# A memory-recurrent transformer block: a planner that counts TensorE's instructions, and the first 16 recurrent steps cut into parts

## The chip, the core and the metric

The kernel runs on one core of a Trainium2 chip. The core has TensorE (matmuls, PE in the profile; its weight loads are PEld), VectorE (DVE), ScalarE (ACT), GpSimd (POOL) and SyncE (SP, which here issues nearly all DMAs). Each engine runs its own instructions in order and waits on semaphores for the others. TensorE can be cut into tiles (two of 64 rows, four of 32 columns, eight of 64 x 32), which work beside each other. Results go to PSUM, eight banks of 128 x 512 float32, and are copied from there to SBUF by ScalarE or VectorE. The metric is the device time of one execution in microseconds (us), as a median of runs.

## What is computed

Two layers, each an attention with a recurrent memory (A) followed by a gated MLP (B), with the same weights in both layers:

```python
for s in range(n_seg):                                  # 64 segments of 32 rows
    h = jnp.concatenate([mem, xs], axis=1)              # 8 memory rows + 32 rows of x
    q, k, v = (jnp.einsum('btd,dhe->bhte', h, W) for W in (Wq, Wk, Wv))   # 16 heads of 256, D = 448
    scores = jnp.where(mask, jnp.einsum('bhqe,bhke->bhqk', q, k) * scale, -1e9)
    o = jnp.einsum('bhte,hed->btd', jnp.einsum('bhqk,bhke->bhqe', softmax(scores), v), Wo)
    mem = o[:, :M, :]                                   # the next segment's memory
    outs.append(o[:, M:, :])
...
x = x + A(layernorm(x)); x = x + B(layernorm(x))        # B: (relu(x Wg) * (x Wu)) Wd, 1792 wide
x = x + A(layernorm(x)); x = x + B(layernorm(x))
```

The memory rows make the segments of a layer a chain: segment s + 1 cannot start its memory part before segment s has put out its eight memory rows.

## The kernel before

*Weights folded.* At the start the kernel multiplies Wq with Wk to `A` and Wv with Wo to `Bsb` for each head (`weights`, `values`, lines 828 and 842), so that a step needs the scores h A h' and the output P h B alone. The first two steps (`step < RAW`) use Wv and Wo one after the other (`unfused`), since `Bsb` isn't ready. The MLP's weights are loaded into the space that the staging of these weights leaves free (`glu_weights`: 18 loads, each of which waits for the one before it).

*The chain.* `chain(step)` is one step of the recurrence, for both layers at once: the second layer runs LAG = 7 segments behind the first, so that there are 70 steps. Step by step: the u pass (line 1021: two halves of 56 matmuls, 7 blocks x 4 column tiles x 2 row tiles, of `mT`, the transposed memory, with `A`); the copy of its four PSUM parts to `Usb`; `turn_u`, which transposes them on VectorE into `uT` (the last 32 columns by way of `tl`); `middle`: scores (line 1228), softmax, its transpose to `PTm` (507, 513), the y product (1286, 1289) and its copy to `YTm`; the output pass (line 1063: 56 matmuls of 448 columns in four column tiles, into one bank `bo`); its copy as a high and a low bfloat16 part, `Ohi` on ScalarE and `Olo` on VectorE, with a small copy of each; the column sums with `Sel` (line 493, 8 matmuls into the bank `br`), which give the transposed memory; and its copies to `mT` (one on VectorE, two across the halves of the partitions) and to `mC`, whose transpose `Rsb` goes to the memory rows of later segments by copies and DMAs. Other segments' rows ride along in the columns that the memory leaves free (`ride`, `single`, `third`; tiles `Tr`, `Pr`, `Tsb`).

*The rest of the work.* All other rows of the segments (`att_half`, `att_group`), the MLP (`glu_units`, `glu_down`) and the norms depend on the chain by the memory rows only. This work fills TensorE while a step's copies and softmax run.

*Who sets the order.* Every operation is recorded with what it reads and writes, a cost per engine and a priority (`_Sched.add`). TensorE's order is written out: `LINE` says, one sign per matmul group, which of the groups left comes next. The orders of the other engines, and which engine takes a copy that several may take (`EV`: ScalarE or VectorE), follow in `schedule()` from the planned times and priorities; `ORDER` shifts the priorities of parts. Where the plan sees a long hole on TensorE, it puts in dummy matmuls (`filler`, line 1646). A change of the tile shape costs `TURN` in the plan. `emit` writes out each engine's instructions with the waits.

Of the kernel before, what the change touches and what calls it, by code (L numbers as in the profile page):

```python
# [7 lines left out]
ACT = mybir.ActivationFunctionType  # L8
# [4 lines left out]
D = 448  # L13
# [3 lines left out]
M = 8  # L17
# [15 lines left out]
ORDER = ("rtaaaaRrjSAaQuLYRAnSb0LNYORXJTwUURBAoZFYxGIsOlyBLeuISxkqYlTuxwENNFHCQAvHZCKfIDDPxGVOqz0UgvrawGAaGoiaLCUaExvfad"  # L33
         "apaqZXakeoayYiaOYeYk0uvaahTxSJfZrbspHeSjbFsgCWHFsi00NtwfOraapajVAgpBxWpieejwMdTNGrdneahPhAIzaaraqrHfIpFMQpkxhC"
         "CcZZkDSqlpyOjQzgeHnQUhcuSapdaFmhKRdiOYlpiweLwTmPA0smp0JM0yggNJbZbTKZbfDNlluCEsJoSYVLqXjxxtjWPavwaZkADUurYfyFcq"
         "fkO0aVDSSVDLhdmLTjENTFZUoRixmDKTKaCaalbXJUbaNAosqbfRysAGdJDHgjAXgUSiugIKbjRFcMfkV0oxwbAjuwihxEaHjLXxAe0kIvNKaU"
         "datURQkpwEDKLvfzvSc0YIogTIaApWBDxUZJeNgmOJtkAXhjaZoaRCADL0LnFXXoujjvuSklKPoKBWwaXSOGFsQdAyPwKbhlUjkVqZRftprce0"
         "sSZoMXrRLmVXlac0aLSlIVcyMitQzKXyHLgcVPWyXgdgoKwHNodXtuYRLkSbrYuaAEabcvgehdwCVIHfiRrbgDCLkuYzcGZAgSTAAJmcynUVhk"
         "HVyeIEYlmbAgeixIMWfqccp0UvwwaLDaURdrT0sKsBd0OXyIoaUvOLUVtEuDaTKlwhOs0IDxsOKOSDaBOaeTWgzTRMfEwZlnGJZxPTLRgnPAcz"
         "pPBQyVXZgVLCFGybysTTGTh0mCnasZeIVJLcWhMbZfRaPDaNK0QMEBqrAXpkhODS0SZRhmQoKZJAGnpKlAZfVagMNVdHcaqsaMZiuKdQvwgmVj"  # L40
         "GFHUajftyotDaeMNKnYfbsoNMGdKptSpckDOFvzlRcjHjMhZJknKkfgUrdanHaZpYHaaXSzQuocWelk0EthLJTCBIlvuZygRbQqPoCYXjKaEda"
         "oNQIcpihSMTRhRAAsqTNXbjwwRSbmlJeFEyMrmhNtZtsmcNunW0Emio0hEayjLtmvrtYBkgaRXXabaxxY0IUKljBSaaaaaaQkHsKaXaaaaaaaa"
         "aaaaaaaaaaadII0lNPSanJakbnc")

SIGNS = "ABCDEFGHIJKLMNOPQRSTUVWXYZabcdefghijklmnopqrstuvwxyz0123456789+-*/=<>()[]{}.,:;!"
LINE = ("AAEACAABAHHFDDDBAAAAIHEDECBAABAJHHCEBDAAAIAIHDBBCAAAAHIHGCCAABAAHIHGDECCBAKAIHAEBCBAAIAPHoJHAABDCCAAAeAdABALCA"
        "XRAEUAKSA~bAQAPAnOAcMALAAJABHAGAgTBADXACABAAAGWAFSCEVQGAFUODGMACGJPGOOGCHFCFAHDMBECDBABAGAAABTAACCPASWBHJAXKAA"
        "IOAAAHOFAFAQPAABBLCQSAAIIACGGGHGH=SR6GXQYFPFCNAAAANJJJLKKJAIIAACFLAEADAAFGAAAAECAANBBLOYAAQAAHJRMAAAEEAODFAUUE"
        "=.aASFBBBOCAMAAAJJJ5JJKKAsJPAIHHAGGGAFBGGEADDAABGBAAAABCAAAAKYQAVdAIaJAHEPAAAGDDDAAMBBbaEBADCAUaAACRAQCBARNNNA"
        "ALAML43LRArJJBIBHHHAGAIHeAGAACDCCGAAAAADBAATMAAWWedKVAaJJfAvAtKcLKAAAElJVADDA44FF1CCz5GABBDAcsbrjChoooGAAlXADD"  # L50
        "jjAABgelLBVbb(b7AaaabKCZBXAXWGAATAYAAQEAOhOOOEDAOMFKAWLKFhEYHHAALFMRFWMLFFFiAQKFEAssHRHQDAmOIAAiGGgAjfffAAdAfe"
        "AEAZAZfAAXBA2UUAAARRRtRAzTSDBDDBAALAAAGHMAFFfFFFAHADAAPBCCBZYBoKPVL0KZBwMBWMLBBBFKFBEMBhDA=/FuEAB<8BEBB4ACk1bB"
        "ayyyAZfAuAAvuQ~BrirAwgPEnBmlACjjjkLANgGggfAAdjAAAaBRAXyGWWWCYCUCTUUTldCSAAZACUObDNCAAvDJJJEDWKVLKHAzyAFEANtAGA"
        "qvBpQFEmmmBBkkFAjjJFggAAGdC[c(cccdFAAZADCYYAAAVTAAYSRlRkAQQQRDQCCCBAAJAVbAAAfSdTjSbVFAQAEDQzZDAAKKBTBxILBBBFFB"
        "EAA=/DlCc9FiC*KCAB2WA0iAAxxxAAwvAvvukQbAqwhPPAAAkBoCimBhhhAgAgfQWDAbIgAAuY1YzYYYACXWAWqAVVU1DCAYREAADNrNTRCMMM"
        "LAMEJAm22EUUHDxA2AXuEAOEq~FDpppApCEmCDDlkAAAhDAAedBcAADZZZaAAXABAWWAAARSwoSRAVrQBCDDCBAJJJKAAAGAAARXAACbBiZBBL"
        "dLLBTZ5BMvB1MBBBILnMLBUqEAA**CJCC<8cABBA3k2kEDzzzAzAxAxxfAAuRArhqhpQsAnnnPCAlkElkBApiNYfBeAdAAAAZZZAAaYXAAWWDf"
        "DAASEAAPUOOUCCMMMAOAKDAH98CPOG4A9MAE0RzZ2yyyADOwvAvuUCCrAwKQEAEl;l:DkkkAFAihAihE4DeAdMAADAYDCWAAAAARRRSAgFDACA"
        "AAJAXAAAFAYofFRcRGFPEAQAATBYOKBVLBrNBBBLuVFBEAA<=fFC-CcA=B7BD5AlC2223kC10AAyyAAfvR0AVs,s.RvAqqqGqSoOBBDAjjAAhA"
        "AAejIAcHSHZZZAbAIWAjXXBBBA-TRYAAQAOOFRAMMMEASKR77DAHOA2BBaEZxADvPuuuvAAsAttAAJQpnAAAlAFji,AAgggD(EDAdFbAADDZZX"  # L60
        "AAAVAAAYSRmRkAQQQBACCNAALAJAVAaAAnnSedSSAETYQS0SzEEOAvDQVMALAvB2B0LKBBBFFIBrIH65EBZACCCFxCCA0u~LAtVQQqqq~CAqpP"
        "RooFCtmDCjaiCYgBAeeeKEAbbAbbFRCYeCCAVATTtCBRRRERmEEANAaFNNMcAAIAIOHDaGZGfCLFFFIIAQEADHsrDRGGAmABqkGLiAhhhFQAfA"
        "dDcdcAAAZDAAWbAAU0ATTTUAARASRxoAXQPrGCCMCLBBAIIIEEAFFACYRAAcBaiBNAeNMBAKZSKAK1A0KApIAAAIkIApDA--FICC7CA-a4AD2l"
        "1112kDzA0zAFATA1uAAsQqqiQooopAPPlmAAAllDhCAAgmAdmAdAbGaAKYYYZQYXAYnYYAAUAMTZSC+BQADO{DRNNNDNxMMAWVLAAAYRAYBAOF"
        "AMELLLMAEKJAIKJEAAGFAEADXDDDEAABLAOAHSGaAFBOAHTHHDJPDAAAFCEECGCABAHCCAAAAABCAFAGEEEADAAB")


class _Op:
    __slots__ = ("idx", "engs", "cost", "fn", "deps", "prio", "dma", "eng", "ndep", "users", "ready",
                 "start", "end", "need_inc", "val", "clock", "slot", "seq", "alloc", "mode",  # L70
                 "touch", "busy", "cross", "at", "also", "land", "side", "group")
# [1730 lines left out]
```

## Time and profile before

| | |
|---|---|
| median of 3 runs | 1491.38 us (1491.05 to 1492.07) |
| the profiled execution | 1486.13 us, of which the span from the first to the last instruction 1484.3 us |
| granted TensorE clock | 1.000 over the whole span |
| instructions | 79353 |
| VectorE, ScalarE, GpSimd busy | 78%, 62%, 12% of the span |
| matmuls | 35104, and as many weight loads |

A matmul is put down with the time from its start until its result is in PSUM, so that several overlap, and a busy TensorE need not be at its full rate. Idle time of an engine stands in square brackets with what ended it; "issue" is idle time in which the engine waited for nothing that the profile shows. Times in a timeline, and in the chain of waits, count from the start of the span.

### The profile page before, as it was taken

To read this page: it belongs to the slowest core of one execution; us is meant where nothing else is said; L and a number is where in the kernel's file an instruction comes from. 1 tells how busy PE (TensorE), PEld (TensorE's weight loads), DVE (VectorE), ACT (ScalarE), POOL (GpSimd) and SP (SyncE) were. 2 spreads that over 40 slices of the span, in tenths; PEclk is the share of its full clock that TensorE was granted. 3 is DMA by queue.
4 is the path that set the end of the run, shared out by engine and by line. 5 is a ranking of instruction groups with operands and counts; after the bars stand their busy time and mean duration, and the time that the engine had idled before them with its cause. 6 is when DMAs were issued, how large, how long until landed. Compare 5 with 4: busy or idle time off the path is not lost.

```text
span 1484.3 us, 79353 instructions
## 1 busy us (share of the span) xinstructions
PE 1459.1 (98%) x35104; PEld 1031.4 (69%) x35104; DVE 1151.0 (78%) x3862; ACT 915.4 (62%) x2635; POOL 179.6 (12%) x701
## 2 busy tenths in 40 slices
PE   9998999999999999999999999999999999999999
PEld 6555666677767776777768767677668676776676
DVE  6677777788877878687877878697887878778865
ACT  7766666676656667566656656575665657556553
POOL 3011111111111111011110111011110111011000
PEclk9999999999999999999999999999999999999999
DMA  9502200000000000000000000000000000000000
GB/s 275 152 26 65 59 8 9 9 9 8 9 4 14 9 8 15 4 17 5 18 4 14 8 11 11 4 18 5 17 5 8 14 11 12 4 11 5 11 9 12
DMA packets 64552, 34.00 MB, mean 23 GB/s; under 512 B 34112, under 2 KB 64080, under 8 KB 64208
## 3 DMA queue, kind: packets, MB, share of 16 engines
q1 hardware_dynamic: 63888, 28.65, 7.7%
q8 instruction: 276, 4.52, 1.3%
q14 instruction: 68, 0.56, 0.1%
q10 hardware_dynamic: 320, 0.26, 0.1%
HBM read 21.36 MB, written 1.84 MB: 16 GB/s over the span
## 4 chain that ended last, share of the span: by engine, by line
PE 92%; DVE 4%; ACT 1%; DMA 1%; issue 1%; SPq 1%; POOL 0%
PE psG L493 22%; PE psG L1374 15%; PE psC L1063 10%; PE psG L1581 9%; PE psC L1021 8%; PE psG L1021 5%; PE psG L1286 3%; PE psG L1063 2%; PE psG L1400 2%; PE psG L1610 2%; PE psG L842 2%; PE psC L1228 1%; PE psC L1286 1%; PE psC L493 1%; PE psG L828 1%; PE psC L1374 1%
## 5 line engine op out<-in xcount | busy, mean ns | idle before, releaser
L493 PE MATMUL psG<-Bsb,P 128*128 128x448 bf16 x1232 | 262.2, 353 | 0.0
L1374 PE MATMUL psG<-HT,A 64*128 64x128 bf16 x4388 | 254.9, 216 | 0.3 <-issue 0.3
L1374 PE MATMUL psG<-HX,A 64*128 64x128 bf16 x3291 | 238.6, 216 | 0.0
L1374 PEld LDWEIGHTS psG<-HT,A 64*128 64x128 bf16 x4388 | 210.5, 94 | 7.8 <-issue 2.3
L483 ACT ACTIVATE Ug<-psG 64x128 bf16<-64x128 f32 (+4 forms) x405 | 142.6, 369 | 61.1 <-PE psG L1374 35.8
L1374 PEld LDWEIGHTS psG<-HX,A 64*128 64x128 bf16 x3291 | 173.8, 94 | 0.0
L493 PEld LDWEIGHTS psG<-Bsb,P 128*128 128x128 bf16 x1232 | 107.2, 97 | 92.6 <-issue 9.3
L1063 PE MATMUL psC<-Bsb,YTm 128*32 128x448 bf16 x3080 | 156.0, 353 | 0.7 <-ACT YTm L483 0.4
L1212 DVE STREAM_TRANSPOSE uT<-Usb 128x384 bf16<-128x384 bf16 x280 | 144.3, 536 | 0.3 <-PE psC L1228 0.3
L1021 PE MATMUL psG<-A,mT 64*32 64x448 bf16 x4032 | 141.8, 350 | 1.4 <-ACT mT L483 0.5
L1021 PE MATMUL psC<-A,mT 64*32 64x448 bf16 x3808 | 136.6, 350 | 1.1 <-issue 0.9
L1581 PE MATMUL psG<-GG,glu 64*128 64x256 bf16 x2310 | 133.6, 269 | 0.0
L486 DVE CAST Ug<-psG 64x128 bf16<-64x128 f32 (+4 forms) x284 | 112.6, 407 | 19.8 <-PE psG L1374 8.5
L1581 PEld LDWEIGHTS psG<-GG,glu 64*128 64x128 bf16 x2310 | 111.6, 94 | 16.3 <-issue 1.5
L1063 PEld LDWEIGHTS psC<-Bsb,YTm 128*32 128x32 bf16 x3080 | 77.7, 97 | 61.5 <-issue 3.0
L483 ACT ACTIVATE P<-psG 128x448 bf16<-128x448 f32 x219 | 111.5, 543 | 7.5 <-PE psG L1289 2.6
L1021 PEld LDWEIGHTS psC<-A,mT 64*32 64x32 bf16 x3808 | 70.4, 92 | 51.5 <-ACT mT L483 5.6
L493 PE MATMUL psG<-glu,P 128*128 128x448 bf16 x434 | 94.2, 352 | 0.3 <-DMA glu<-in_B_W_down_dram 0.3
L1021 PEld LDWEIGHTS psG<-A,mT 64*32 64x32 bf16 x4032 | 74.1, 92 | 25.2 <-ACT mT L483 2.9
L1592 DVE TENSOR_TENSOR P<-P,psG 128x512 bf16<-128x512 bf16 x82 | 56.3, 686 | 41.6 <-ACT P L1591 41.2
L1591 ACT ACTIVATE P<-psG 128x512 bf16<-128x512 f32 x83 | 49.5, 596 | 62.6 <-PE psG L1581 56.0
L486 DVE CAST P<-psG 128x448 bf16<-128x448 f32 x130 | 78.8, 616 | 10.3 <-PE psG L1289 8.8
(282 smaller groups left out, 3160.9 us busy)
## 6 DMA issues: line engine op xcount, KB each, us to landing
Tsb<-Rsb SPq DMA_DIRECT2D x288, 1.5 KB
Tsb<-Rsb SPq DMA_DIRECT2D x288, 2.0 KB
HR<-xn SPq DMA_DIRECT2D x128, 32.0 KB, 1.9
Bsb<-in_A_Wq_dram SPq DMA_DIRECT2D x6, 384.0 KB, 6.8
Bsb<-in_A_Wk_dram SPq DMA_DIRECT2D x6, 384.0 KB, 6.3
HR<-Rsb SPq DMA_DIRECT2D x126, 1.5 KB
HR<-Rsb SPq DMA_DIRECT2D x126, 2.0 KB
X<-in_A_x_dram SPq DMA_DIRECT2D x16, 112.0 KB, 3.2
```

The source lines that it names most:

```text
L483: return E.activation(out, i, ACT.Copy, scale=1.0 if scale is None else scale)
L486: return E.tensor_copy(out, i)
L493: return E.matmul(out, lhsT=lhsT, rhs=rhs, **k)
L842: i = E.matmul(bk.ap()[row0:row0 + mn, to:to + of.stop - of.start], lhsT=lhs[:, et, m0:m0 + mn], rhs=rhs[:, et, of], start=(et == 0), stop ...
L1021: i = E.matmul(ub[v].ap()[32 * j:32 * j + 32, 0:D], lhsT=self.mT[rw, WHERE[b], first:first + 32], rhs=cols, start=(b == 0), stop=(b == 6), ...
L1063: x = E.matmul(bo.ap()[32 * j:32 * j + 32, 0:D], lhsT=self.YTm[:, q, :], rhs=self.Bsb[:, chunks[q], :], start=(i == 0), stop=(i == 13), ti ...
L1212: self.s.add("dve", 560, busy=486.0, fn=lambda E, e, v=v, of=of: E.transpose(outs[:, 2 * v:2 * v + 2], of), r=[("Usb", 2 * half + v)], w=[ ...
L1286: return E.matmul(ps[:, n * q:n * q + n], lhsT=HR[rows, 128 * q:128 * q + 128], rhs=PT, start=True, stop=True, tile_position=(b, 0))
L1374: i = E.matmul(ub[v].ap()[:, 128 * n:128 * n + 128], lhsT=self.A[rw, b, a0:a0 + 128], rhs=HT[rw, WHOLE[b], :, 0:SEG] if CROSS[b] is None e ...
L1581: i_ = E.matmul(two[v].ap()[:, 256 * c:256 * c + 256], lhsT=self.Wgu[rw, b, f0:f0 + 128], rhs=self.GG[rw, :, WHOLE[b] if CROSS[b] is None ...
L1591: s.add("act", ev_cost(512)["act"], lambda E, e, dst=dst, z=z: E.activation(dst, z(0), ACT.Relu), r=[two[0]], w=w, room=old)
L1592: s.add("dve", dv_cost(512), lambda E, e, z=z, dst=dst: E.tensor_tensor(dst, dst, z(1), ALU.mult), r=[two[1]], w=w)
```

## The change

It has three parts.

1. *The plan.* `count()` runs every TensorE operation once with a stand-in that counts matmuls, and puts down two instructions for each. `schedule()` keeps a lead: how far the instruction stream is ahead, at most `AHEAD` = 500 ns. Each TensorE operation adds its time and takes `ins` times 11.5 ns from it (16 ns between 88 and 135 us of planned time); where the lead falls below zero, the operation's planned time grows by what is missing. `ORDER` and `LINE` are written anew for the new plan and the new operations.
2. *The first 16 steps* (`step < EARLY`). The output pass is done in two column pieces of 320 and 128 columns, the second in a bank of its own (in steps 0 and 1 one bank, and only the copies are in pieces). Each piece has its high and low copy. The column sums are done in two groups with a bank each, where the first needs the first piece alone, and the copies to `mT` and `mC` are in two groups as well. The first half of the u pass is three operations (blocks 0, 2; 1, 3; 4, 5, 6), of which the first two need the first group's copies only. The second half of the u pass is copied and turned in two groups of 224 columns. In steps with one active chain, y goes to two banks (256 and 192 columns).
3. *The start.* 15 warming matmuls in place of 18.

```diff
+    FETCH = (11.5, 16.0, 88000.0, 135000.0)
+    AHEAD = 500.0
...
+    def count(self):
+
+        for o in self.ops:
+            if "pe" in o.engs:
+                for h in o.touch:
+                    h.name = self.pools[h.pools[0]][0]
+                c = _Count()
+                o.fn(c, o.mode if o.also else "pe")
+                o.ins = 2 * c.n
...
     def schedule(self):
+        self.count()
+        lead = self.AHEAD
...
                 t0 = max(t0, free[e] + turn)
                 o.start = t0
+                lead = min(self.AHEAD, lead + t0 + c - free[e] - o.ins * self.FETCH[self.FETCH[2] < t0 < self.FETCH[3]])
+                c -= min(lead, 0.0)
+                lead = max(lead, 0.0)
                 free[e] = t0 + c
...
+CUT = 320
+LAST = [("mTb", c) for c in range(2)]
+LASTX = [("mTc", v) for v in range(2)]
+EARLY = 16
...
-            for _ in range(18):
+            for _ in range(15):
...
+            for bs, mk in (((0, 2), MEM), ((1, 3), cross), ((4, 5, 6), LAST + LASTX)) if early and half == 0 else whole:
+                def fn(E, e, half=half, ub=ub, bs=bs):
+                    for b in bs:
...
+            for gs in ((0,), (1,)) if early and half == 1 else ((0, 1),):
+                n = 224 * len(gs)
...
+                self.turn_u(half, gs, P)
...
+        pieces = [(bo, 0, 0, D)]
+        if step < EARLY:
+            b2 = bo if step < RAW else self.bank("C", "G")
+            pieces = [(bo, 0, 0, CUT), (b2, CUT if step < RAW else 0, CUT, D)]
+        for bk, c0, d0, d1 in pieces if step >= RAW else ():
+            for lo, hi in ((0, 5), (5, 10), (10, 14)) if not early else ((0, 7), (7, 14)) if d0 == 0 else ((0, 14),):
...
+        for n, (bk, c0, d0, d1) in enumerate(pieces):
...
+            s.add("act", ev_cost(w)["act"], lambda E, e, ps=ps, o=o: E.activation(hi_[:, o], ps(), ACT.Copy), r=[bk], w=[("Ohi", n)], **P)
+            s.add("dve", dv_cost(w), lambda E, e, ps=ps, o=o: E.tensor_tensor(lo_[:, o], ps(), hi_[:, o], ALU.subtract), r=[bk, ("Ohi", n)], w=[("Oli", n)], **P)
...
+        for n, ks in enumerate(((0, 1), (2, 3)) if early else ((0, 1, 2, 3),)):
+            br = self.bank("C", "G")
...
+            ok = [("Ohi", 0), ("Oli", 0)] if early and n == 0 else [("Ohi", i) for i in range(len(pieces))] + [("Oli", i) for i in range(len(pieces))] + ["Oh2", "Ol2"]
...
+        two = len(act) == 1 and c1 == 1 and m["n"] == "m"
+        yb = [self.bank("C", "G") for _ in (0, 1)] if two else [self.bank("C", "G") for _ in act]
```

243 lines of the change are left out of this document (134 added, 109 removed).

## The prediction

> **What bounds the kernel now.** I read the first part and the chain part of the page, then the busy times by stage, then the chain of waits through one early step and through the one place where it runs over a DMA, and last the timeline of one step's end.
>
> ```profile
> span 1484.3 us, 79353 instructions
> ...
> PE 1459.1 (98%) x35104; PEld 1031.4 (69%) x35104; DVE 1151.0 (78%) x3862; ACT 915.4 (62%) x2635; POOL 179.6 (12%) x701
> ...
> PE 92%; DVE 4%; ACT 1%; DMA 1%; issue 1%; SPq 1%; POOL 0%
> ```
>
> By stage (start and end, length, then busy time and instructions of TensorE, its weight loads, VectorE, ScalarE and GpSimd, the granted clock, the DMA share and GB/s):
>
> ```profile
> 88.00:135.00 47.00, 40.62 (x1060) 24.89 (x1051) 35.81 (x146) 30.29 (x92) 7.72 (x31) 1.00 0.17 44
> 135.00:230.00 95.00, 88.25 (x2464) 59.09 (x2461) 71.91 (x270) 56.87 (x170) 12.68 (x52) 1.00 0.15 38
> 230.00:331.00 101.00, 97.83 (x2614) 70.20 (x2607) 82.05 (x295) 66.94 (x207) 13.82 (x55) 1.00 0.04 9
> 331.00:660.00 329.00, 328.18 (x7981) 233.85 (x7986) 259.81 (x875) 205.05 (x607) 39.85 (x159) 1.00 0.04 10
> ```
>
> TensorE sets the end. From 331 us on it is idle for 0.82 us of 329: there only less TensorE work saves time. Between 88 and 331 us (steps 2 to 15) it idles 6.38 + 6.75 + 3.17 = 16.30 us. Dummy matmuls are counted as busy, so the loss is somewhat larger:
>
> ```profile
> L1646 PE MATMUL psG<-A x28: 349/353/363, 102.5 to 305.6; 128*128 128x448 bf16 x28
> ...
> 156.44 1.12 PE L1646 MATMUL psG<-A 128*128 128x448 bf16 x5
> ```
>
> Five dummies last 1.12 us, the last one 0.35, so one is worth (1.12 - 0.35) / 4 = 0.19 us and the 28 of them 5.3 us. Some 21 us in all is what a faster recurrence could win in these steps. Step 4 shows where they go, in the chain of waits (start, length, what):
>
> ```profile
> 127.81 1.55 PE psG L1021 x56
> 129.39 0.62 DVE Usb L486
> ...
> 132.64 0.27 PE psC L1228 x4
> ...
> 135.15 0.55 ACT YTm L483
> ...
> 135.75 2.83 PE psC L1063 x56
> 138.58 0.14 PE psC L513
> ...
> 139.29 0.56 DVE Olo L1070
> ...
> 139.87 0.19 DVE Olo L1072
> ...
> 140.11 0.36 PE psG L493 x8
> ...
> 140.54 1.53 PE psG L1479 x98
> 142.07 1.04 PE psG L1021 x33
> ```
>
> The output pass ends at 138.58 and the column sums start at 140.11: 1.53 us of copies, with no useful matmuls but a pair. In the order of instructions steps 4, 5, 6, 10 and 14 have at most 17 short matmuls there besides dummies; steps 2, 3, 7, 8, 9 and 13 have a cover of 1.0 to 1.6 us; steps 11, 12 and 15 are covered. Then the sums are copied before the next u pass may start:
>
> ```profile
> 138.63 0.55 ACT L1069 ACTIVATE Ohi<-psC 128x448 bf16<-128x448 f32 x1 [2.15 <-PE psC L1063]
> 139.21 0.62 DVE L1070 TENSOR_TENSOR Olo<-psC,Ohi 128x448 bf16<-128x448 f32 x1
> 139.87 0.18 DVE L1072 COPY Olo<-Olo 128x64 bf16<-128x64 bf16 x1
> 140.51 0.19 DVE L1087 CAST mT<-psG 128x32 bf16<-128x32 f32 x1 [0.46 <-PE psG L493]
> 140.73 0.18 DVE L486 CAST mT<-psG 64x24 bf16<-64x24 f32 x1
> 140.95 0.28 ACT L483 ACTIVATE mC<-psG 128x128 bf16<-128x128 f32 x1
> ```
>
> One place in these steps is held by something else. In SyncE's timeline:
>
> ```profile
> 123.03 0.65 SPq L785 DMA_DIRECT2D glu<-in_B_W_up_dram  x1
> ...
> 128.52 0.73 SPq L785 DMA_DIRECT2D Tsb<-Rsb  x1
> 129.30 0.60 SPq L785 DMA_DIRECT2D glu<-in_B_W_up_dram  x1
> ...
> 160.13 3.01 SPq L785 DMA_DIRECT2D Tsb<-Rsb  x4
> ```
>
> and in the chain of waits:
>
> ```profile
> 163.18 5.15 DMA glu<-in_B_W_down_dram
> ...
> 168.34 3.29 DMA glu<-in_B_W_down_dram
> ...
> 171.67 0.55 PE psG L493 x2
> 172.23 1.80 PE psC L1063 x33
> ```
>
> The MLP's weights arrive one load after the other, and the last lands at 171.63; the two matmuls that need it stand ahead of step 6's output pass (172.23) in TensorE's order, as they do in the changed order.
>
> **The change, part by part.** *Plan and order.* No instruction is added by the count itself. The two built programs differ in tile-shape changes on TensorE by 561 to 559, behind the 16th step by 386 to 381, and the matmuls there are the same: I take nothing for everything behind step 15 (ends -1 and +1, about the 0.82 us of idle time there). Dummies go from 38 to 18 (28 of them are the row above); they stand in waits and are no term of their own.
>
> *Start.* 18 warming matmuls become 15.
>
> ```profile
> 1.22 5.43 PE L735 MATMUL psC<-P 128*128 128x448 bf16 x18 [1.22 <-DVE cvec L765]
> 4.93 1.28 PEld L735 LDWEIGHTS psC<-P 128*128 128x128 bf16 x7 [0.22 <-issue]
> ```
>
> The last seven go at 1.28 / 7 = 0.18 us, so three fewer bring the first transposes forward by 0.5 us if their weights are there: -0.5 (ends -0.6 and 0).
>
> *Output pass in two pieces*, 56 matmuls of 320 columns and 56 of 128 in place of 56 of 448 at 2.83 - 0.18 = 2.65 us. The 320 scale to 320/448 of it, 1.90. For the 128 the nearest rows are dense runs of 98 short matmuls, good and bad:
>
> ```profile
> 59.00:60.80 1.80, 1.60 (x98) 1.49 (x98) 1.00 0.98 306
> ...
> 108.49 0.20 PE L1479 MATMUL psG<-HX,A 64*128 64x64 bf16 x2 [1.35 <-issue]
> ```
>
> Their weight loads are busy for 1.49 us: 1.49 / 98 = 15 ns each where the instruction stream was ahead, as again in step 4 (1.53 us for 98). The same 98 starved for 1.35 us at 108.49, so (1.49 + 1.35) / 98 = 29 ns each. 56 of them cost 0.85 to 1.62 us, the pass 2.75 to 3.52: +0.10 to +0.87 per step. I take +0.2 (the good rows are the more numerous behind 135 us), ten times from step 6 on: +2.0 (ends +1.0 and +8.7). [...]
>
> *What the pieces bring.* The 0.55 and 0.62 us copies behind the pass shrink to those of 128 columns: 0.28 on ScalarE (the mC row has 128), and on VectorE 0.19 + (96/416) x 0.43 = 0.29. The small copy of 0.18 hangs on the first piece alone. If VectorE has just finished the first piece's low part, 1.53 becomes 1.53 - 0.27 - 0.33 - 0.18 = 0.75; that part (0.50 by the same slope) starts some 0.5 us behind the first piece's end and may hold it, so 0.95: -0.6. The new wait is that of the second group of sums on the second low part; behind it on TensorE stand four of seven rounds of the next u pass, which need the first group alone.
>
> *Sums in two groups, u pass in parts.* A u half is 56 matmuls in about 1.33 us (2.77 for the 112 at 142 us), so 4/7 of one, 0.76 us, runs while the second group is copied (140.51 to 140.91). Less one or two tile changes I take -0.6. *u copies by groups:* 224 columns for 448 take 0.62 to about 0.39 on VectorE, at the cost of two more copies: -0.2. *y in two banks*, in steps 0 to 6 alone: 256 columns for 448, about -0.15 each; these steps lie before the landing, so I count nothing.
>
> *More instructions elsewhere:* ScalarE 2515 to 2624, VectorE 3864 to 3911, over 16 steps; at 0.2 to 0.3 us each that is about 45 us over the two engines in 280 us that they fill to 60 and 76%. On the path I take +1.5 (ends 0 and +5).
>
> *The sum.* (a) Start -0.5. (b) To step 6's output pass every gain ends in the wait for the landing at 171.63. SyncE's order in the changed program puts the load of 129.30 ahead of the Tsb transfers that it waited behind (its predecessor was issued 6.3 us earlier, at 123.03), and the one of 163.18 behind two of them: up to -3.0 and -1.2. The loads cannot start before the last weight product, which has some 2 us more work ahead of it in the new order. I take -2.5 (ends -4.5 and +2). A transfer that waits for TensorE also moves ahead of one such load; it is in the ends. (c) Steps 6 to 15: three fully exposed (6, 10, 14) win 0.6 + 0.6 + 0.2 = 1.4 each, four half covered (7, 8, 9, 13) 0.6 each, three nothing: -6.6; pieces +2.0, copies +1.5: -3.1. In all -0.5 - 2.5 - 3.1 = -6.1 us. The profiled execution took 1486.13 us, 1.83 around its span; the span goes to 1478.2 and that execution to 1480.0. The median of the runs shown, 1491.38, is 5.25 above it; I keep that distance: 1485.3.
>
> **The rivals.**
>
> *The stream starves (slower).* In the output pass of the first 16 steps TensorE takes twice the instructions for the same columns. If the 128-column piece runs at 29 ns everywhere, it costs +0.87 x 14 = 12.2; with the gains of 6.6, copies of 1.5 and nothing at the landing the sum is +7.1 - 0.5: 1498. For it: the starved row at 108.49. Against it: both 15 ns rows, the later one from a step behind it. It decides from (6.6 + 0.5 - 1.5) / 14 = 0.4 us per step on.
>
> *The landing eats it (no change).* If step 6 stays at 172 and the copies take 4 instead of 1.5, -0.5 - 0.6 = -1.1: 1490.3. For it: 171.63 stands ahead in both orders, and steps 11, 12 and 15 have nothing to win.
>
> *All of it counts (much faster).* If VectorE holds nothing up, 2.0 per exposed and 1.0 per half covered step from 6 on are -10, the landing -4.5: with pieces +1.0 and start -0.5 that is -14: 1477. Against it: the idle and dummy time is 21 us in all, a third of it before the landing.
>
> *A floor per short matmul (about no change).* If matmuls in column tiles of 32 go no faster than the u pass's, 1.33 / 56 = 24 ns, the 128-column piece takes 1.33 us for my 0.95: +3.8, 1489.1. For it: no row shows one in such tiles below that. Against it: 15 ns in the larger tiles. [...]
>
> **How the numbers follow.** Chances: forecast 0.45, starving 0.22, landing 0.18, all 0.11, floor 0.04. 0.2% is 3 us, about what a measurement can tell from no change. Faster (under 1488.4): most of the forecast's, 0.38, and 0.11, with a little of the landing's: 0.51. Same: 0.21. Slower: starving, and the forecast's tail with copies at 5: 0.28. The forecast's own range is 1479 to 1492; with the starving case the range is 1476 to 1498.
>
> **What would show it.** Step 16's u pass begins here now:
>
> ```profile
> 331.55 0.36 PE L1021 MATMUL psC<-A,mT 64*32 64x448 bf16 x1
> ```
>
> Right: the second sums start 0.9 to 1.1 us behind the output pass in steps 4, 5, 10 and 14; the u pass follows the sums within 0.3 us; the 128-column matmuls in 0.8 to 1.0 us; the last weight load lands at 167 to 170 and TensorE waits there; that row stands at 324 to 327 us, and the distance from there to the end is the same. Wrong: "issue" waits in the output pass beyond 135 us, sums that wait for the first piece's low part, or a landing behind 172.

## The result, and the profile after

| | before | after |
|---|---|---|
| median of 20 runs each | 1491.16 us (1486.58 to 1496.85) | 1488.12 us (1485.70 to 1490.71) |
| ratio | | 0.998, 95% interval 0.9971 to 0.9989 |
| profiled execution | 1486.13 us, span 1484.3 | 1487.06 us, span 1485.2 |
| granted TensorE clock in it | 1.000 | 0.998 |

The changed kernel is 3.0 us faster in the median (1.6 to 4.3 us by the interval), 2.8 us above the forecast of 1485.3 and inside the range of 1476 to 1498, which is wide enough to hold the time before as well. The two profiled executions do not show this gain. The one of before was faster than all 20 timed runs of its kernel and 5.0 us below their median; the one of after lies 1.1 us below its own. So the profiles serve here to show where time moved inside a step, and the medians to show how much of it there was.

The head of the page of after, and its chain:

```profile
span 1485.2 us, 81070 instructions
...
PE 1461.7 (98%) x35865; PEld 1043.0 (70%) x35865; DVE 1155.6 (78%) x3909; ACT 931.3 (63%) x2744; POOL 181.5 (12%) x712
...
PE 93%; DVE 5%; issue 1%; ACT 1%; DMA 0%; SPq 0%; POOL 0%; POOLq 0%
```

The windows of the prediction, now in after (start and end, length, busy time and count of TensorE, its weight loads, VectorE, ScalarE and GpSimd, the clock, the DMA share, GB/s):

```profile
88.00:135.00 47.00, 41.63 (x1076) 26.79 (x1072) 37.91 (x156) 31.81 (x104) 8.39 (x35) 0.95 0.21 52
135.00:230.00 95.00, 87.89 (x2806) 64.72 (x2796) 75.80 (x295) 61.46 (x209) 15.13 (x62) 0.99 0.14 35
230.00:331.00 101.00, 99.09 (x2963) 75.58 (x2968) 85.99 (x318) 71.21 (x235) 13.97 (x57) 1.00 0.05 9
331.00:660.00 329.00, 328.36 (x7993) 234.26 (x7982) 260.29 (x875) 205.24 (x609) 38.95 (x154) 1.00 0.05 10
```

TensorE idles 5.37 + 7.11 + 1.91 = 14.4 us between 88 and 331 us, for 16.3 before: little of the idle time went away. The first two clocks are below 1, which they were not before.

**What the change does where little covers the wait.** The end of step 10 on TensorE (start, length, what, in brackets the idle time ahead and what ended it), first before, then after:

```profile
235.81 2.83 PE L1063 MATMUL psC<-Bsb,YTm 128*32 128x448 bf16 x56 [0.24 <-DVE YTm L486]
...
238.99 0.73 PE L1646 MATMUL psG<-A 128*128 128x448 bf16 x3
240.16 0.19 PE L493 MATMUL psG<-Sel,Ohi 128*128 128x32 bf16 x1 [0.44 <-DVE Olo L1072]
...
240.35 0.18 PE L493 MATMUL psG<-Sel,Olo 128*128 128x32 bf16 x1
240.46 0.34 PE L1286 MATMUL psC<-PTr,HR 40*128 40x128 bf16 x6
...
241.18 0.76 PE L1021 MATMUL psG<-A,mT 64*32 64x448 bf16 x24 [0.32 <-DVE mT L486]
```

```profile
233.99 2.87 PE L1112 MATMUL psC<-Bsb,YTm 128*32 128x320 bf16 x112
236.91 0.40 PE L526 MATMUL psG<-ident,xn 128*128 128x128 bf16 x4
237.22 0.19 PE L526 MATMUL psG<-Sel,Ohi 128*128 128x32 bf16 x1
...
237.77 0.19 PE L526 MATMUL psC<-Sel,Ohi 128*128 128x32 bf16 x1 [0.29 <-DVE mT L1148]
...
237.86 0.18 PE L526 MATMUL psC<-Sel,Olo 128*128 128x32 bf16 x1
237.96 0.36 PE L1062 MATMUL psC<-A,mT 64*32 64x448 bf16 x1
```

From the start of the pass to the next u pass it took 5.37 us and takes 3.97. The u pass follows the second sums by 0.10 us, where it stood 0.83 behind the last sum for the copies. This is a gain of 1.40 us, the size that the prediction gave an exposed step. Ten short matmuls of y (240.46 to 240.86) filled part of the wait before, and stand elsewhere in after. The second sums end their wait on VectorE's copy of the first group to `mT`, which stands right behind the second low part. The other two steps that the prediction called fully exposed did otherwise: from the start of the pass to the next u pass, step 14 takes 0.5 us less and step 6 0.5 us more. So 1.40 times the number of exposed steps is not what steps 6 to 15 gained together.

### The profile page after: what moved, and what is told of

Its sections match the earlier page's. It is cut to its first block, busy times and chain, and to the rows that moved or that the text cites. A ratio compares the mean times of both kernels' runs of the same rounds, so it can differ in the third digit from the quotient of the medians.

```text
span 1485.2 us, 81070 instructions
## 1 busy us (share of the span) xinstructions
PE 1461.7 (98%) x35865; PEld 1043.0 (70%) x35865; DVE 1155.6 (78%) x3909; ACT 931.3 (63%) x2744; POOL 181.5 (12%) x712
## 4 chain that ended last, share of the span: by engine, by line
PE 93%; DVE 5%; issue 1%; ACT 1%; DMA 0%; SPq 0%; POOL 0%; POOLq 0%
PE psG L526 23%; PE psG L1444 15%; PE psC L1112 10%; PE psC L1062 9%; PE psG L1651 9%; PE psG L1062 4%; PE psG L1680 3%; PE psG L1356 3%; PE psG L1470 2%; PE psG L879 2%; PE psC L1356 1%; PE psC L1295 1%; PE psG L865 1%; PE psG L1112 1%; PE psC L526 1%; PE psC L1444 1%
## 5 line engine op out<-in xcount | busy, mean ns | idle before, releaser
L1444 PE MATMUL psG<-HT,A 64*128 64x128 bf16 x4392 | 259.1, 217 | 1.3 <-DVE P L519 0.8
L1444 PEld LDWEIGHTS psG<-HT,A 64*128 64x128 bf16 x4392 | 215.0, 94 | 8.7 <-issue 3.1
L1444 PEld LDWEIGHTS psG<-HX,A 64*128 64x128 bf16 x3294 | 178.4, 94 | 0.3 <-issue 0.2
L1112 PE MATMUL psC<-Bsb,YTm 128*32 128x448 bf16 (+2 forms) x4032 | 172.2, 323 | 0.8 <-issue 0.7
L1062 PE MATMUL psG<-A,mT 64*32 64x448 bf16 x4004 | 160.1, 350 | 0.9 <-issue 0.8
L1062 PE MATMUL psC<-A,mT 64*32 64x448 bf16 x3836 | 155.2, 350 | 1.2 <-issue 0.8
L1112 PEld LDWEIGHTS psC<-Bsb,YTm 128*32 128x32 bf16 x4032 | 94.9, 97 | 60.7 <-issue 3.1
L1062 PEld LDWEIGHTS psC<-A,mT 64*32 64x32 bf16 x3836 | 80.5, 93 | 58.0 <-ACT mT L516 5.5
L519 DVE CAST Ug<-psG 64x128 bf16<-64x128 f32 (+4 forms) x276 | 108.9, 404 | 13.7 <-PE psG L1444 7.2
L516 ACT ACTIVATE P<-psG 128x448 bf16<-128x448 f32 x207 | 106.1, 546 | 9.4 <-PE psG L1359 7.8
L1062 PEld LDWEIGHTS psG<-A,mT 64*32 64x32 bf16 x4004 | 82.3, 93 | 19.0 <-issue 2.5
```

Of the source, the lines that this page charges most:

```text
L516: return E.activation(out, i, ACT.Copy, scale=1.0 if scale is None else scale)
L519: return E.tensor_copy(out, i)
L1062: i = E.matmul(ub[v].ap()[32 * j:32 * j + 32, 0:D], lhsT=self.mT[rw, WHERE[b], first:first + 32], rhs=cols, start=(b == 0), stop=(b == 6), ...
L1112: x = E.matmul(bk.ap()[32 * j:32 * j + 32, c0:c0 + d1 - d0], lhsT=self.YTm[:, q, :], rhs=self.Bsb[:, chunks[q], d0:d1], start=(i == 0), st ...
L1444: i = E.matmul(ub[v].ap()[:, 128 * n:128 * n + 128], lhsT=self.A[rw, b, a0:a0 + 128], rhs=HT[rw, WHOLE[b], :, 0:SEG] if CROSS[b] is None e ...
```

## Where it went

I cut each step into a front (from the first matmul of its u pass to the first of its output pass), the pass (to 0.30 us behind the start of its last matmul) and a tail (from there to the next u pass). The sums of the windows view over the ten fronts and the ten tails of steps 6 to 15 say how much TensorE was busy, and the same for the dummy matmuls alone. In this order: tails, dummies in them, fronts, dummies in them. Before:

```profile
sum 31.88, PE 28.60; mean PE 2.86
sum 31.88, PE 2.91; mean PE 0.29
sum 112.52, PE 108.91; mean PE 10.89
sum 112.52, PE 1.10; mean PE 0.11
```

After:

```profile
sum 25.56, PE 23.02; mean PE 2.30
sum 25.56, PE 0.70; mean PE 0.07
sum 117.34, PE 113.27; mean PE 11.33
sum 117.34, PE 1.49; mean PE 0.15
```

| steps 6 to 15, us | before | after | difference |
|---|---|---|---|
| tails | 31.88 | 25.56 | -6.32 |
| of which useful work (busy less dummies) | 25.69 | 22.32 | -3.37 |
| of which idle or dummies | 6.19 | 3.24 | -2.95 |
| output passes (the rest) | 27.80 | 30.45 | +2.65 |
| fronts | 112.52 | 117.34 | +4.82 |
| of which useful work | 107.81 | 111.78 | +3.97 |
| of which idle or dummies | 4.71 | 5.56 | +0.85 |
| step 6's u pass to step 16's | 172.20 | 173.35 | +1.15 |

The tails became 6.3 us shorter, nearly what was forecast. But half of that is other work which stood in them and now stands in the fronts, where it takes much the same time. By these cuts, waiting fell by 2.95 us in the tails and rose by 0.85 in the fronts, and the two column pieces cost 2.65.

The cut behind the pass treats a last matmul of 128 columns, which takes 0.22 us, like one of 448, which takes 0.35. Cut at the last result instead, the ten passes are 1.4 us longer and the tails 5.1 us shorter; the fronts stay as they are.

The longer fronts are not an accident of one execution of after. Seven other kernels below keep this order and the parts in steps 6 to 15, but for the u copies in two of them (plan_uncounted, more_dummies, shaken, copies_whole, fat_early, no_dummies, dummies_whole). Their tails take 25.1 to 26.0 us, their fronts 117.1 to 120.4, and the whole from step 6's u pass to step 16's 172.3 to 176.6. (In plan_uncounted and no_dummies a half-clock stretch lies within; without these two, 118.5 and 175.8 are the most.) Of the kernel before there is only the one profile, with 172.2.

## The experiments

None leaves out a part of the computation. Ratios are against the kernel before, run on the same chip in the same rounds. The rows plan_uncounted to one_piece and more_dummies shared rounds and chip, and so did shaken to sums_wait, the two orders, and the last two; the changed kernel was not run again beside any of them. So medians compare best within such a group. "U16" is the start of step 16's u pass in the profiled execution, 331.55 us before and 329.68 after. "Half clock" is how long the clock stood at 0.5 ahead of U16, behind the start, in that execution; before had none.

| kernel | median, us (runs) | ratio, 95% interval | U16 | half clock, us | clock of the runs, mean |
|---|---|---|---|---|---|
| after | 1488.12 (20) | 0.998 (0.9971 to 0.9989) | 329.68 | 6.8 | 0.9985 |
| plan_uncounted | 1487.67 (12) | 0.9992 (0.9979 to 1.0005) | 334.57 | 6.8 | 0.9991 |
| u_whole | 1489.27 (11) | 1.0002 (0.9991 to 1.0012) | 333.86 | 3.4 | 0.9978 |
| one_piece | 1496.34 (5) | 1.0038 (1.0026 to 1.005) | 338.81 | 0 | 0.9992 |
| more_dummies | 1486.04 (10) | 0.9977 (0.9968 to 0.9986) | 330.23 | 0 | 0.9992 |
| shaken | 1488.75 (11) | 0.9998 (0.9983 to 1.0012) | 330.45 | 3.4 | 0.9983 |
| copies_whole | 1487.51 (11) | 0.998 (0.9967 to 0.9993) | 333.30 | 6.8 | 0.9986 |
| fat_early | 1491.84 (11) | 1.0011 (0.9999 to 1.0024) | 333.58 | 3.4 | 0.9990 |
| sums_wait | 1495.93 (5) | 1.0041 (1.0025 to 1.0056) | 341.24 | 13.7 | 0.9978 |
| old_order | 1505.02 (5) | 1.009 (1.0072 to 1.0107) | 349.49 | 13.7 | 0.9958 |
| new_order | 1499.65 (6) | 1.0053 (1.0036 to 1.007) | 343.43 | 6.8 | 0.9990 |
| no_dummies | 1490.35 (12) | 0.9999 (0.9986 to 1.0011) | 334.14 | 6.8 | 0.9973 |
| dummies_whole | 1490.06 (12) | 0.9998 (0.9986 to 1.001) | 331.62 | 0 | 0.9985 |

**The plan without its count.**

```diff
-    FETCH = (11.5, 16.0, 88000.0, 135000.0)
+    FETCH = (0.0, 0.0, 88000.0, 135000.0)
```

> The changed kernel, with the instruction count taken out of the plan again (both fetch prices 0); TensorE's written order stays, the plan then sees longer holes and puts in 40 dummies for 18. My theory: the gain comes from the shorter recurrence, not from the count: 1487 to 1489 us like the changed kernel's 1488.1, and with more dummies rather no stretch at half clock (the changed kernel's profile has two of 3.4 us). Rival: the count places work and copies where the stream is short, and without it the time goes back by 2 us or more, to 1490 and above, with more issue waits between 88 and 331 us.

The median is that of the changed kernel within the spread; the ratio is one the interval of which includes 1, since the runs of before beside it were faster too. U16 is 4.9 us later, with as much half clock ahead of it as in after, where the theory had expected rather none. The run takes out the count and adds 22 dummies, so it does not tell the two apart. The count by itself is not shown to pay or to cost in the median.

**The u pass waits for all copies again** (all early steps but 1 and 6).

```diff
-            for bs, mk in (((0, 2), MEM), ((1, 3), cross), ((4, 5, 6), LAST + LASTX)) if early and half == 0 else whole:
+            for bs, mk in (((0, 2), MEM), ((1, 3), cross), ((4, 5, 6), LAST + LASTX)) if early and half == 0 and step in (1, 6) else [(bs, whole[0][1]) for bs in ((0, 2), (1, 3), (4, 5, 6))] if early and half == 0 else whole:
```

> The changed kernel, where the three parts of the first u half all wait for all copies of the memory again (not in steps 1 and 6, where the written order puts a part ahead of the second sums). My theory: from the last sum to the u pass 0.8 to 0.9 us instead of 0.11 in the exposed steps; 3 us or so more at step 16's u pass and in the time (1490 to 1492). Rival: the wait is hidden or moves, and the time stays within 1.5 us of the changed kernel's 1488.1.

In steps 2, 3, 9, 10 and 13 the u pass stands 0.73 to 0.91 us behind the sums instead of 0.11. The part of the change does what it says, and is worth 0.6 to 0.8 us where the sums are followed by the u pass. In the time it is worth less than my theory said: the median is 1.2 us above the changed kernel's, within the rival's range, and 1.6 above that of plan_uncounted in the same rounds. The ratio to the kernel before is 1, but so is that of the control below (shaken), which takes nothing out.

**One piece again** in steps 2 to 11 and 13 to 15 (448 columns, rounds 0 to 4, 5 to 9, 10 to 13 at the three places of the pieces).

```diff
-        if step < EARLY:
+        if step < EARLY and (step < RAW or step == 12):
             b2 = bo if step < RAW else self.bank("C", "G")
...
-            for lo, hi in ((0, 5), (5, 10), (10, 14)) if not early else ((0, 7), (7, 14)) if d0 == 0 else ((0, 14),):
+            for lo, hi in ((0, 5), (5, 10), (10, 14)) if not early or len(pieces) == 1 else ((0, 7), (7, 14)) if d0 == 0 else ((0, 14),):
```

> The changed kernel with the output pass of steps 2 to 15 (but 12) in one piece of 448 columns again; the sums stay in two groups, both behind the whole pass. My theory: the pass is 0.17 us shorter, the wait from it to the second sums goes from 1.1 back to about 1.9 us; net 0.6 us more per exposed step, 2 to 4 us in all (1490 to 1492). Rival: the pieces only add instructions, and one piece is faster by about 14 x 0.17 = 2 us (1486).

The pass falls back from 2.65 to 2.48 us. In steps 2, 3, 6, 9, 10 and 14 the second sums move from 1.0 to 1.2 us behind the start of the last output matmul to 2.2 to 2.5. U16 comes 9.1 us later, and the median is 8.7 us above that of plan_uncounted in the same rounds. The pieces are worth more in this order than I gave them.

**More dummies**: a hole is filled from 100 ns on and to 95%, for 300 ns and 80%; 50 dummies for 18.

```diff
-                n = int((t0 - free[e] - 300.0) * 0.8 / ns)
+                n = int((t0 - free[e] - 100.0) * 0.95 / ns)
```

> The changed kernel with dummies in holes from 0.1 us on (for 0.3) and up to 95% of them (for 80%): 50 for 18. My theory: the two stretches at half clock in the changed kernel's profile come of too little TensorE work in the early waits and cost up to 1.7 us each; with the dummies the clock is 1.000, step 4's output pass takes 2.65 us for 4.11, and the time is 1485 to 1487. Rival: the stretches are chance or come anyway, and dummies that overrun their hole cost: 1488 or more.

The lowest median of all, and no stretch of low clock ahead of the last microseconds of the profiled execution. Its interval overlaps that of the changed kernel, so it is not shown to be faster than that one. It gives the output pass of step 4 at full clock:

```profile
133.73 2.58 PE L1112 MATMUL psC<-Bsb,YTm 128*32 128x320 bf16 x91
137.00 0.49 PE L1112 MATMUL psC<-Bsb,YTm 128*32 128x128 bf16 x21 [0.69 <-issue]
```

The last 21 short matmuls had to wait 0.69 us with nothing that the profile shows to wait for, with the clock at 1. I call this starving, as the rival did; that an instruction stream was late is not shown. So the pass takes 3.54 us, where the theory had said 2.65.

**A constant of the plan moved by 8 ns**, as a control.

```diff
-    PE_END = 162.0
+    PE_END = 170.0
```

> The changed kernel with one constant of the plan moved: a matmul's end is planned 8 ns later (PE_END 170 for 162). TensorE's matmul order and the work are the same; the order on VectorE, ScalarE and GpSimd and the dummies are laid out anew. Theory A (the parts of the change set the time): within 1 us of the changed kernel in the median, and step 16's u pass at 329 to 331 us. Rival B (where the plan happens to put copies of other work, such as the MLP's norm in step 6, is worth as much as a part of the change): step 16's u pass 1.5 us or more away from 329.7, with step 6 nearer to 21.5 than to 19.6 us or another step longer by a microsecond or more.

U16 is 0.8 us later and step 6 lasts 20.85 us for 19.61, nearer to rival B's 21.5. By the median and U16 theory A held: new places for the copies are worth about a microsecond here. But the ratio to before is 1 within its interval, while the changed kernel's was 0.998: differences of 2 us between medians of ten runs taken at different times, on different chips, are not to be read.

**The u sums copied and transposed whole.**

```diff
-            for gs in ((0,), (1,)) if early and half == 1 else ((0, 1),):
+            for gs in ((0, 1),):
```

> The changed kernel with the u sums copied and transposed whole again (448 columns in one copy, not in two groups of 224), as before the change; pieces, sums in two groups and u parts stay. The prediction took -0.2 us per exposed step for the groups and +1.5 us on the path for all additional copies. Theory A: u pass to scores gets 0.1 to 0.3 us longer in steps 6, 10 and 14, but VectorE and ScalarE lose some 30 instructions each, so the whole is within 1 us of the changed kernel. Rival (the additional copies are what ate the gain of steps 6 to 15): steps 6 to 15 shorter by 1 to 3 us, median 1485.5 to 1487.

Within 1 us in the median, as theory A said. Steps 6 to 15 did not get shorter (175.8 us for 173.35), so the rival, that the additional copies ate the gain, is not borne out.

**One piece in steps 2 to 5 alone.**

```diff
-        if step < EARLY:
+        if step < EARLY and not RAW <= step < 6:
...
-            for lo, hi in ((0, 5), (5, 10), (10, 14)) if not early else ((0, 7), (7, 14)) if d0 == 0 else ((0, 14),):
+            for lo, hi in ((0, 5), (5, 10), (10, 14)) if not early or len(pieces) == 1 else ((0, 7), (7, 14)) if d0 == 0 else ((0, 14),):
```

> The changed kernel with the output pass of steps 2 to 5 in one piece of 448 columns (three groups of rounds, so that TensorE's order keeps its places). Theory (the instruction stream starves in the second piece there): step 4's pass lasts 2.5 us at full clock, for 3.5 to 4.1, but the sums start 2.0 to 2.4 us behind the pass for 1.1, so step 6's u pass comes at 156 to 158 us, within a microsecond of the changed kernel, and the median is within 1.5 us of it. Rival (the long pass of step 4 is the half clock alone, or starvation just moves on to the next short matmuls): the pass is 2.5 us but issue waits of the same sum stand in front of the next u pass or the attention's short matmuls, and step 6 comes 1 to 2 us later.

Step 4's pass lasts 2.48 us, for 4.11 in after, where half the clock lies over it, and 3.54 at full clock with more dummies. So the extra time came with the second piece, the theory's first half. The second half fell: step 6 comes at 161.28 us, 5 us later, though after has two half-clock stretches ahead of there and this execution one. The median is 3.1 us above that of shaken in the same rounds. Starving included, the two pieces still pay in steps 2 to 5 of this order.

**Both groups of sums wait for all copies.**

```diff
-            ok = [("Ohi", 0), ("Oli", 0)] if early and n == 0 else [("Ohi", i) for i in range(len(pieces))] + [("Oli", i) for i in range(len(pieces))] + ["Oh2", "Ol2"]
+            ok = [("Ohi", 0), ("Oli", 0)] if False else [("Ohi", i) for i in range(len(pieces))] + [("Oli", i) for i in range(len(pieces))] + ["Oh2", "Ol2"]
```

> The changed kernel with both groups of column sums waiting for all copies of the output pass; pieces, u parts and copies by groups stay. Theory A (the first group's early start is worth its place: its copies run while the second group waits): the first sums start 0.5 us later in steps 4, 5, 6, 10 and 14, the u pass follows 0.1 to 0.4 us later than in the changed kernel, step 16's u pass 331 to 333 us, median 1489 to 1491. Rival (the second low part is the last wait in any case, so nothing is lost): the second sums start at the same 1.0 to 1.2 us behind the pass and step 16's u pass stands within 1 us of 329.7.

The second sums start 1.46 to 1.54 us behind the start of the last output matmul in steps 2, 3, 6, 10 and 14, for 1.03 to 1.24, and the median is 5 us above the upper end of theory A; U16 is 11.6 us later, 3.6 of it already at step 2. This execution has 6.8 us more of half clock ahead of U16 than after, which can be 3.4 of the 11.6 (half of it, an estimate). The direction is that of theory A, the size far above it.

**The parts and the order apart.** The last three showed losses of several microseconds when one part is taken out, more than the whole change brings. So the parts were put into the order of before, and the order was put onto the kernel before, in one and the same way: TensorE's written order and the priorities exchanged, with each split operation at the place of the whole one and the reverse. (Only the two tables `ORDER` and `LINE` differ from after and from before.)

> The changed kernel's operations (pieces, two groups of sums, u parts, copies by groups, the count) in the order of the kernel before: TensorE's order is the one of before, each split operation's parts standing one behind the other at its place, and the priorities (ORDER) are those of before. Theory A (the parts win in the exposed waits as the prediction priced them, whatever the order): step 16's u pass 3 to 6 us earlier than before's 331.55, at 325.5 to 328.5 us, median 1485 to 1488. Rival B (parts and order belong together: where other work stands in the waits already, a shorter wait is worth nothing): step 16's u pass within 1.5 us of 331.55 or later, median 1489.5 to 1493.

> The kernel before (one output pass of 448 columns, one group of sums, whole u passes, no count) in the order of the changed kernel: TensorE's order is the changed one, each whole operation standing where the last of its parts stood (the output pass's three groups of rounds at the places of the pieces, those of step 12 in rising order), with the priorities of the changed kernel. Theory A (the new order takes cover out of the waits, which only the parts' shorter waits allow): step 16's u pass 4 us or more later than before's 331.55, at 336 to 342 us, median 1494 or more. Rival C (the order brings the gain by itself, by moving the weight loads forward and the work to better places): step 16's u pass at 329 to 331.5 us, median 1487 to 1490.

| U16, us | order of before | order of after |
|---|---|---|
| whole operations | 331.55 | 343.43 |
| parts of the change | 349.49 | 329.68 |

Theory A of the first kernel and rival C of the second fell. Rival B has the direction, with a median 12 us above the range that it named; the second's theory A held in the median and was exceeded by 1.4 us in U16. Each half by itself loses, 8.5 and 13.8 us in the medians, together they win 3. In the parts in the old order the wait behind the output pass shortened in three of the five steps that the prediction had called uncovered: the second sums stand 1.09, 1.14 and 1.55 us behind the start of the last output matmul in steps 4, 6 and 10, where the same columns' sums stood at 1.99. In the other two, 5 and 14, it did not (2.67 and 2.02). In the half covered steps 7, 8 and 9 they moved back to 2.15, 2.78 and 2.37, where other work stands between the pieces and the sums. Part of the losses is the clock: the half clock ahead of U16 can be 6.8 of 17.9 us in the parts in the old order, and 3.4 of 11.9 in the whole operations in the new one (half of the stretches, an estimate).

The whole operations in the new order show what the order does by itself. In the tails of steps 6 to 15 useful work falls from 25.7 to 22.5 us, and in the fronts it rises from 107.8 to 111.5. Without the parts, idle time and dummies in these tails rise from 6.2 to 12.8 us. With the parts and the count, in after, they are 3.2. So the order takes the cover out of the waits, and the rest of the change takes out the waits that are then bare: some 9.5 us of them, more than the 6.2 that were there to save before.

**Dummies.** Without any, all else in the same order; and, as a try for a faster kernel, more of them with whole u copies.

```diff
-            if e == "pe" and (begun or done > 1):
+            if False:
```

> The changed kernel without any of its 18 dummy matmuls behind the warming ones; all other work and its orders as in the changed kernel. Theory D (fewer dummies let TensorE's clock fall to a half for stretches of 3.4 us in the early steps; the change took 38 dummies down to 18): the mean granted clock of the executions falls below the 0.9985 of the changed kernel, to 0.996 to 0.998, two to four stretches in the profile before 331 us, median 1489 to 1491. Rival (dummies that stand in waits are worth nothing, and the stretches come whatever stands there): mean clock 0.998 to 0.999 and the median within 1 us of 1488.1.

> The changed kernel with more dummies in its waits (as in the run with 50) and the u sums copied and transposed whole (as in the run that undid their groups). If the two add up, each on its own having stood at 1486.0 to 1487.5: a median of 1484.5 to 1486.5 and a ratio to the kernel before of 0.995 to 0.9975, clock 0.999 or more. If the order of copies laid out anew decides instead: within 1 us of 1487.5, ratio 0.998 or above.

With 0, 18 and 50 dummies the mean clock of the runs is 0.9973, 0.9985 and 0.9992, and the median 1490.35, 1488.12 and 1486.04. In these three the clock goes as theory D said. The number of dummies alone does not set it: the kernel before has 38 and a mean clock of 0.9980 in the 89 runs beside the experiments, below the changed kernel with 18. The medians go the same way, but they come from different rounds, 2 us apart, a difference that the control says is not to be read. In the one comparison within the same rounds, dummies_whole, with 52 dummies and a clock of 0.9985, lands at 1490.06, for 1490.35 without any. So the two gains do not add up, and how much of the time the dummies or the clock explain stays open. No kernel here is shown to beat the changed one.

## Why the prediction was right, and where it was not

*The number was in range, its working less so.* The sum was made against the profiled execution: span 1478.2 us. It measured 1485.2. The distance from there to the median was kept at 5.25 us and was 1.06. The first error is 7.0 us, the second 4.2 the other way. That most of it cancelled is luck: the profiled execution before was 5.0 us faster than its median, the one after 1.1, and nothing in the prediction gave a reason for that. The 7.0 us divide into 0.2 up to step 6's output pass, 4.0 in steps 6 to 15 and 2.8 behind.

*Start, -0.5.* Not found in this execution:

```profile
1.22 5.78 PE L772 MATMUL psC<-P 128*128 128x448 bf16 x15 [1.22 <-DVE cvec L802]
...
6.90 0.68 PE L865 MATMUL psG<-ident,Bsb 128*128 128x128 bf16 x8
```

15 warming matmuls took 5.78 us where 18 had taken 5.43. In the profiles of the eleven other kernels with 15 they took 4.33 to 5.43 us, 4.8 in the mean, and in the other kernel with 18 5.59. So the term stands on average, within a spread from execution to execution that is larger. The clock's record begins, with 1, at 7.08 us in after and at 5.01 in before.

*Up to step 6's output pass, -2.5.* Right in size and in the load, wrong in the wait. SyncE's issues of the two last loads, with the transfer of the last of them (KB, us from issue to landing), and TensorE around it:

```profile
159.99 0.43 SPq L822 DMA_DIRECT2D glu<-in_B_W_down_dram  x1
...
164.82 0.45 SPq L822 DMA_DIRECT2D glu<-in_B_W_down_dram  x1
```

```profile
glu<-in_B_W_down_dram SPq DMA_DIRECT2D x1, 224.0 KB, 2.7
```

```profile
167.60 0.92 PE L526 MATMUL psG<-glu,P 128*128 128x448 bf16 x4
...
168.78 0.55 PE L526 MATMUL psG<-glu,P 128*128 128x448 bf16 x2
169.39 2.09 PE L1112 MATMUL psG<-Bsb,YTm 128*32 128x320 bf16 x56
171.29 0.97 PE L1112 MATMUL psC<-Bsb,YTm 128*32 128x128 bf16 x56
```

The load lands at 164.82 + 2.7 = 167.5, 4.1 us earlier than before (forecast 167 to 170), and the pass starts at 169.39 for 172.16: -2.77. But TensorE no longer waits for it: it is busy up to the two matmuls that need the load, at 168.78. The gain is there already at step 6's u pass, 156.33 us for 159.35. The rival in which the landing eats the gain fell with that.

*The pieces, +2.0.* Right in size: +2.65 in steps 6 to 15 from first start to last start, of which 1.12 is step 7. To the last result, which is how the prediction's 2.83 - 0.18 counted, it is +1.4, of which 1.0 is step 7: a pass without an issue wait takes 2.87 us for 2.83, 0.04 more and not 0.2. There the short piece takes 0.97 us, as in the rows above, latency included, near the price by the good row of before. The floor of 24 ns per short matmul would have made it 1.33; it fell, with 56 of them in 0.97 us. The issue waits of the starving rival came in two places: in step 4, as the rows of more_dummies show at full clock, and in step 7, which has "issue" ahead of its last matmuls, named as a sign against the forecast:

```profile
185.96 2.08 PE L1112 MATMUL psG<-Bsb,YTm 128*32 128x320 bf16 x56
187.86 0.63 PE L1112 MATMUL psC<-Bsb,YTm 128*32 128x128 bf16 x30
189.21 0.57 PE L1112 MATMUL psC<-Bsb,YTm 128*32 128x128 bf16 x26 [0.73 <-issue]
```

It did not come everywhere, and so never decided. Waits of TensorE for nothing shown, 135 to 331 us, total, count and longest, before and after:

```profile
PE psG L1286 <- issue: 0.7, 1, 0.7
...
PE psG L1479 <- issue: 0.5, 2, 0.3
...
PE psG L1610 <- issue: 0.2, 1, 0.2
```

```profile
PE psC L1356 <- issue: 1.6, 2, 1.1
PE psC L1112 <- issue: 0.7, 1, 0.7
...
PE psG L1680 <- issue: 0.4, 1, 0.4
PE psG L1062 <- issue: 0.3, 1, 0.3
...
PE psG L1470 <- issue: 0.3, 1, 0.3
```

1.4 us became 3.3: not in the passes alone but in the short y matmuls of step 7's front (L1356), too.

*The gains of steps 6 to 15, -6.6, and the copies, +1.5.* This is the step that failed. In step 10 the way from the pass to the u pass did shrink by 1.4 us, and the ten tails by 6.3. But the prediction booked the shortening of the tails as time saved. There were only 6.19 us of waiting and dummies in these tails to save; the "21 us in all" counted the fronts and the steps ahead of the landing with them. In the new order the tails hold 3.4 us less work, and the fronts 4.0 more: that, more than any new waiting (0.85), made up most of the 4.8 us by which the fronts grew. Steps 6 to 15 came to +0.9 from step 6's output pass on, for -3.1. The row that should have stood at 324 to 327 us:

```profile
329.68 1.52 PE L1062 MATMUL psC<-A,mT 64*32 64x448 bf16 x56
```

*Single signs.* The second sums stand 0.8 to 1.0 us behind the end of the pass in steps 4, 10 and 14 (forecast 0.9 to 1.1), in step 5 1.8, with other work between. The u pass follows within 0.3 us in steps 2, 3, 9, 10 and 13. It comes 0.4 to 0.9 us behind the sums in steps 4, 8, 11 and 12, and 1.8 to 3.0 behind them in 6, 7, 14 and 15, where the attention's short matmuls stand there now. A sign against the forecast came too: in steps 5, 8 and 9 TensorE is idle for 0.59, 0.39 and 0.29 us until the first piece's low part is there for the first sums. And the second sums do not end their wait on the second low part in steps 6 to 10, as forecast, but on the copy of the first group to `mT` behind it, some 0.1 us later in step 10.

*Behind step 15, nothing.* The same work took 1155.5 us for 1152.8. Among the profiles of after and nine variants of it in which all four engines run the same order from 40 us behind U16 on (all but the two orders and shaken), it ranged from 1152.1 to 1156.4. So a difference of this size comes from execution to execution, and the term stands. TensorE's idle time there goes part of the way with it: 1.1 us in dummies_whole, 2.7 in after and 3.9 in fat_early, most of it "issue".

*What stays open.* How the 3 us of the medians divide between the steps: the profiled pair shows 1.9 up to step 16, and single profiles, one for each kernel, do not settle the rest. The clock is a rival for a small part of it. Of the runs beside the experiments, those of the kernel before with a mean clock of 1.000 are 2.0 us faster than those with 0.998 (below); by this the 0.0005 between the mean clocks of the two kernels would be 0.5 of the 3.0 us, an estimate.

## What to carry to other kernels

When a step that the next one needs gets faster, count first the idle time and the fillers that stand in that very stretch. In that order they bound what can be saved; shortening a stretch that holds other work only moves that work. Where an order has been fitted to the operations, taking a part out of the new kernel, or putting it into the old, measures the misfit as well, and here the losses were several times the size of the gain. And a sum made against one profiled execution needs to know where this execution stands among the runs.

## What the runs showed of the hardware

**The clock fell for 3.41 us at a time.** The windows view of after, cut at the two stretches of low clock and the 3.41 us ahead of each (window, length, TensorE busy, clock):

```profile
112.89:116.30 3.41, 1.45 (x77) 1.00 0.25 64
129.96:133.37 3.41, 2.54 (x44) 1.00 0.47 112
```

```profile
116.30:119.71 3.41, 3.40 (x117) 0.50 0.26 64
133.37:136.78 3.41, 3.34 (x55) 0.50 0.31 65
```

Half the clock for 3.41 us each time, and the second begins 17.07 us behind the first, 5.0 times 3.41. In the execution of old_order four such stretches, 13.7 us in all, begin at 124.9, 155.6, 186.3 and 322.9 us. They are 30.7, 30.7 and 136.6 us apart, near 9, 9 and 40 times 3.41.

Ahead of the two falls in after TensorE was busy 1.45 us of 3.41 (43%) and 2.54 (74%); the longest idle times that end there are 1.27 and 0.48 us. In the 3.40 us ahead of falls in three other executions it was busy 1.77 and 1.75 us (no_dummies), 1.28, 1.89, 1.81 and 2.36 (old_order) and 1.34 (shaken). But 1.69 us of 3.40 from 113.6 us on in dummies_whole, and 2.32 from 110.0 on in before, had no half clock behind them. So the busy share alone does not decide in these executions. This is read from the traces, and no run was made to test it; what sets the moment of a fall is not shown.

Among the 89 runs of the kernel before that stood beside the experiments, those with a mean clock of 1.000 have a median of 1487.9 us (10 runs), those with 0.998 one of 1489.9 (34 runs).

**One copy's place.** In step 6 TensorE's order puts the first MLP's transposes (of `xn`) ahead of the next work. VectorE's norm for it stands before the memory's transpose in after, behind it in u_whole (VectorE, then TensorE; after first):

```profile
156.91 0.37 DVE L1383 TENSOR_SCALAR xn<-X,lnst 128x384 bf16<-128x384 bf16 x1
...
157.54 0.40 PE L526 MATMUL psG<-ident,xn 128*128 128x128 bf16 x4
```

```profile
159.57 0.54 DVE L1383 TENSOR_SCALAR xn<-X,lnst 128x64 bf16<-128x64 bf16 x2
...
160.67 0.40 PE L526 MATMUL psG<-ident,xn 128*128 128x128 bf16 x4 [0.25 <-POOL xn L1385]
```

Counted from the step's start (156.33 and 157.71) the transposes come 1.8 us later, 2.96 for 1.21. The step lasts 21.4 and 21.8 us in the two kernels with this order (u_whole and plan_uncounted), and 19.6 in after. But among the nine kernels that keep TensorE's order and have a norm ahead it ranges from 19.6 to 21.5 (one_piece has 21.4 with the transposes at 1.25). So the late transposes are not shown to be what makes the step longer.
